# Score matmuls of two batches behind one another in the second chunk, and a new price for one batch's block, in a gated linear attention with a mixture of experts

## Chip, cores and metric

One NeuronCore of a Trainium2 chip. The metric is the time of one execution on the device in microseconds; the profile's span is some 1.7 us shorter. Verdicts use fast runs only.

## The reference

```python
# attention: B=4, H=8, S=768, D=48
f = 1 / (1 + exp(-f_logit))
for t in range(S):
    state = f[:, :, t, :, None] * state + einsum('bhd,bhe->bhde', k[:, :, t], v[:, :, t])
    y[:, :, t] = einsum('bhd,bhde->bhe', q[:, :, t], state)
# experts: x = y as (3072, 384), E=4, F=1024
p = domain_probs / (domain_probs.sum(-1, keepdims=True) + 1e-09)
out = sum(p[:, e:e+1] * (relu(x @ w1[e]) @ w2[e]) for e in range(E))
```

## The kernel before

The sequence is cut into six chunks of 128 steps. In each, the attention of four batches feeds the expert layers of the chunk. Before the program is built, a list scheduler in the kernel places every operation, with a priority and a price in microseconds, on an engine, and so fixes each engine's order.

```python
class Plan:
    ...
    def run(self):
        # the operation with the best priority that is ready and whose buffers are free goes next
        ...
rooms = {"ps_m": 4, "ps_t": 4, ...}      # PSUM banks: experts, attention

def product(c, b, j, eng): ...   # L276: gated q (j=0) or k (j=1), VectorE or GpSimd

def pe_at(c, b):                 # scores of one batch: 8 matmuls, L300
    QK = tl("QK", c, b)
    for i in range(NP):
        for r in range(2):
            rows = slice(r * P2, r * P2 + D)      # 48 rows from partition 0 or 64
            nc.tensor.matmul(out=tl("A", c, b, r)[:, i, :], lhsT=QK[rows, 1, i, :], rhs=QK[rows, 0, i, :],
                             start=True, stop=True)

def ev_at(c, b, r): ...          # VectorE masks one bank of scores, L304
def pe_y(c, b): ...              # output from scores and state, L311 and L315
def probs(c): ...                # VectorE normalises the expert weights pn, L241 to L244
def mm_h(...): ...               # first expert layer, L344; relu L350 (VectorE), L352 (ScalarE)
def mm_o(...): ...               # second expert layer, L356; ev_o leaves PSUM, scaled by pn: L363, L365, L367
    ...
        pairs = [[b] for b in range(B)] if c < 2 else [[b, b + 1] for b in range(0, B, 2)]
        for bs in pairs:
            at = P.add(f"at {c}.{bs[-1]}", {"PE": 0.4 if len(bs) == 1 else 0.66},
                       lambda e, bs=bs: [pe_at(c, b) for b in bs], slot(bs[-1], 7),
                       deps=[ET[b] for b in bs], takes=[("ps_t", "A", c, b, r) for b in bs for r in range(2)], lag=0.2,
                       frees=[("QK", c, b) for b in bs])
    ...
    done = P.run()
    for o in done:
        o.emit(o.engine)
```

## Time and profile before

| | before |
|---|---|
| time, median of 3 runs | 303.41 us (302.98 to 304.57) |
| span of the profiled run | 302.5 us |
| TensorE busy, granted clock | 97%, full |
| VectorE, ScalarE, GpSimd busy | 45%, 57%, 32% |

TensorE sets the end, so the time changes only where its stream gets shorter or waits. A group in the timeline reads: start, length, engine, line, operation, out<-in, form, count, and in brackets the idle time ahead and what ended it. Matmul ends are modelled and overlap the next start, so what a group costs is read from the start of the next one.

### The profile page before, as it was taken

The page shows a single profiled execution, that of the slowest core. Times are in us where ns is not written, and L with a number is a line of the kernel's source. Part 1 is how long each engine was busy: PE and PEld are TensorE (multiplying, and loading weights), DVE is VectorE, ACT ScalarE, POOL GpSimd, SP SyncE. Part 2 cuts the span into 40 slices and gives each one's busy share as a digit, 9 for nine tenths or more (in the row PEclk, how much of TensorE's full clock was granted, in tenths as well). Part 3 has the DMA queues.
Part 4 walks back from the last instruction along what each step waited for, and adds up shares of the span by engine and source line. Part 5 has one row for each costly group of instructions (what it writes and reads, how often), then busy time and mean ns, then how long its engine had stood idle before and what let it go on. Part 6 is the DMA issues. An engine that isn't in the chain of part 4 may idle for free.

```text
span 302.5 us, 5544 instructions
## 1 busy us (share of the span) xinstructions
PE 294.6 (97%) x2141; PEld 170.9 (56%) x2141; DVE 136.8 (45%) x269; ACT 172.1 (57%) x299; POOL 95.7 (32%) x157
## 2 busy tenths in 40 slices
PE   7898999999999999999999999999999999999995
PEld 5664555566775566556555555555556555555553
DVE  6693002789753574526364426364315253201223
ACT  5766664857776464677455575435566444475440
POOL 4584300407666047332434252622342100000000
PEclk9999999999999999999999999999999999999999
DMA  8999999963995559967799978200422201100003
GB/s 159 206 175 207 208 207 196 218 100 61 216 217 113 113 110 186 179 137 152 141 175 160 220 167 154 50 15 13 115 62 52 48 13 32 66 21 2 0 0 106
DMA packets 137355, 36.10 MB, mean 119 GB/s; under 512 B 128496, under 2 KB 135792, under 8 KB 137328
## 3 DMA queue, kind: packets, MB, share of 16 engines
q1 hardware_dynamic: 131568, 29.45, 49.8%
q0 software_dynamic: 5760, 6.29, 12.5%
q8 instruction: 17, 0.28, 0.4%
q14 instruction: 10, 0.08, 0.1%
HBM read 31.51 MB, written 4.72 MB: 120 GB/s over the span
## 4 chain that ended last, share of the span: by engine, by line
PE 90%; DMA 4%; DVE 3%; POOL 1%; ACT 1%; issue 1%; DVEq 0%; ACTq 0%; POOLq 0%
PE ps_m L356 40%; PE ps_m L344 40%; DMA w_sb<-in_moe_w_dram 3%; PE ps_t L300 2%; PE ps_t L255 1%; PE ps_t L315 1%; PE ps_t L321 1%; PE ps_t L311 1%; POOL qk L276 1%; DMA f<-in_f_logit_dram 1%; DVE qk L276 1%; PE ps_m L569 1%; PE ps_t L285 1%; DVE AT L304 0%; POOL Sf L335 0%
## 5 line engine op out<-in xcount | busy, mean ns | idle before, releaser
L344 PE MATMUL ps_m<-xT,w_sb 128*128 128x512 bf16 (+1 forms) x624 | 153.1, 363 | 1.3 <-DMA w_sb<-in_moe_w_dram 0.9
L356 PE MATMUL ps_m<-w_sb,h 128*128 128x384 bf16 x776 | 153.2, 324 | 0.0
L352 ACT ACTIVATE h<-ps_m 128x512 bf16<-128x512 f32 (+1 forms) x169 | 97.3, 577 | 98.0 <-PE ps_m L344 93.8
L356 PEld LDWEIGHTS <-h 128*128 128x128 bf16 x776 | 73.5, 98 | 58.6
L363 DVE SCALAR_TENSOR_TENSOR o<-ps_m,pn,o 128x384 f32<-128x384 f32 (+1 forms) x73 | 44.6, 611 | 107.2 <-PE ps_m L356 101.3
L344 PEld LDWEIGHTS <-w_sb 128*128 128x128 bf16 x624 | 59.5, 98 | 47.7 <-DMA w_sb<-in_moe_w_dram 1.1
L276 POOL TENSOR_TENSOR qk<-q,e 128x384 bf16<-128x384 f32 x18 | 21.6, 1204 | 64.3 <-ACT e L262 63.9
L350 DVE TENSOR_SCALAR h<-ps_m 128x512 bf16<-128x512 f32 (+1 forms) x39 | 21.9, 578 | 27.1 <-PE ps_m L344 24.2
L304 DVE TENSOR_TENSOR AT<-ps_t,mask 128x512 bf16<-128x512 f32 x48 | 30.2, 682 | 7.4 <-PE ps_t L300 7.4
L335 POOL TENSOR_TENSOR Sf<-Sf,egs 48x192 f32<-48x192 f32 x40 | 20.7, 517 | 39.9 <-DVE Sf L328 37.8
L276 POOL TENSOR_TENSOR qk<-k,e 128x384 bf16<-128x384 f32 x21 | 22.2, 1059 | 20.2 <-ACT e L264 12.9
L262 ACT ACTIVATE e<-ps_t 128x384 f32<-128x384 f32 x24 | 20.7, 864 | 4.8 <-PE ps_t L255 2.6
L328 DVE TENSOR_TENSOR Sf<-Sf,ps_t 48x192 f32<-48x192 f32 x40 | 14.0, 350 | 10.8 <-PE ps_t L321 10.0
L365 ACT ACTIVATE o<-ps_m,pn 128x384 f32<-128x384 f32 x20 | 11.6, 580 | 5.8 <-PE ps_m L356 4.3
L336 POOL CAST sb<-Sf 48x192 bf16<-48x192 f32 x40 | 13.6, 339 | 2.6
L569 PE MATMUL ps_m<-busy 128*128 128x256 bf16 x69 | 12.8, 333 | 1.3 <-DVE busy L140 1.3
L218 POOL CAST vb<-v 128x384 bf16<-128x384 f32 x18 | 9.7, 558 | 11.9 <-DMA v<-in_v_dram 9.7
L264 ACT ACTIVATE e<-ps_t 128x384 f32<-128x384 f32 x24 | 13.0, 541 | 0.0
L247 ACT ACTIVATE ex<-f 128x768 f32<-128x768 f32 (+1 forms) x14 | 10.5, 748 | 3.2 <-DMA f<-in_f_logit_dram 3.2
L315 PE MATMUL ps_t<-vb,AT 128*128 128x48 bf16 x192 | 11.4, 184 | 0.7 <-DVE vb L218 0.7
L315 PEld LDWEIGHTS <-AT 128*128 128x128 bf16 x192 | 9.8, 97 | 2.5 <-issue 0.9
L251 ACT ACTIVATE gp<-ex 128x768 bf16<-128x768 f32 (+1 forms) x14 | 10.5, 751 | 0.4
(50 smaller groups left out, 141.7 us busy)
## 6 DMA issues: line engine op xcount, KB each, us to landing
w_sb<-in_moe_w_dram POOLq DMA_DIRECT2D x8, 768.0 KB, 19.2
out_dram<-o SPq DMA_DIRECT2D x23, 192.0 KB, 2.1
f<-in_f_logit_dram SPq DMA_DIRECT2D x10, 384.0 KB, 4.2
k<-in_k_dram SPq DMA_DIRECT2D x10, 384.0 KB, 5.3
q<-in_q_dram SPq DMA_DIRECT2D x10, 384.0 KB, 5.3
v<-in_v_dram SPq DMA_DIRECT2D x10, 384.0 KB, 5.5
f<-in_f_logit_dram SPq DMA_DIRECT2D x4, 192.0 KB, 3.8
k<-in_k_dram SPq DMA_DIRECT2D x4, 192.0 KB, 4.0
```

Of the source, the lines that this page charges most:

```text
L262: nc.scalar.activation(out=e[:, 0].rearrange("t (d h) -> t h d", d=D), in_=cs[:, 0:HD].rearrange("t (i r d) -> t r i d", r=2, d=D), func=A ...
L276: engines[eng].tensor_tensor(out=tl("qk", c, b)[:, j, :, 0:D].rearrange("t (i r) d -> t i r d", r=2), in0=tl("qk"[j], c, b // 2)[:, hh(b), ...
L304: nc.vector.tensor_tensor(out=tl("AT", c, b)[:, r].rearrange("s i t -> s (i t)"), in0=tl("A", c, b, r).rearrange("s i t -> s (i t)"), in1= ...
L315: nc.tensor.matmul(out=y[:, h * D:(h + 1) * D], lhsT=AT[:, r, i, :], rhs=vb[:, h, :], start=(c == 0), stop=True, skip_group_check=True)
L328: nc.vector.tensor_tensor(out=Sf[rows, b], in0=Sf[rows, b], in1=KV[rows, :, r, :], op=ALU.add)
L335: nc.gpsimd.tensor_tensor(out=Sf[rows, b], in0=Sf[rows, b], in1=eg, op=ALU.mult)
L344: nc.tensor.matmul(out=tl("hp", c, e, fc, n0)[:, n0:n1], lhsT=w1_sb[:, e, kk, fc * 128:(fc + 1) * 128], rhs=tl("xT", c)[:, kk, n0:n1], sta ...
L350: nc.vector.tensor_relu(out=dst, in_=src)
L352: nc.scalar.activation(out=dst, in_=src, func=AF.Relu)
L356: nc.tensor.matmul(out=tl("op", c, e, nt, part)[:, cols], lhsT=tl("h", c, e)[:, fc, nt * T:(nt + 1) * T], rhs=w2_sb[:, e, fc, cols], start ...
L363: nc.vector.scalar_tensor_tensor(out=o, in0=op, scalar=pe, in1=o, op0=ALU.mult, op1=ALU.add)
L569: nc.tensor.matmul(out=spare[:, 0:256], lhsT=busy[:, 0:128], rhs=busy, start=True, stop=True)
```

## The change

It is to give the second chunk what the third to sixth already have: the scores of two batches in one block, so that TensorE changes to the 48-row mode and back twice less. A single block's price is corrected besides.

```diff
-        pairs = [[b] for b in range(B)] if c < 2 else [[b, b + 1] for b in range(0, B, 2)]
+        pairs = [[b] for b in range(B)] if c < 1 else [[b, b + 1] for b in range(0, B, 2)]
...
-            at = P.add(f"at {c}.{bs[-1]}", {"PE": 0.4 if len(bs) == 1 else 0.66}, ...
+            at = P.add(f"at {c}.{bs[-1]}", {"PE": 0.43 if len(bs) == 1 else 0.66}, ...
```

More of the change, by code (lines that the diff above doesn't have):

```diff
@@ L438, in attention @@
             ET[b], VB[b] = et, vb
-        pairs = [[b] for b in range(B)] if c < 2 else [[b, b + 1] for b in range(0, B, 2)]
+        pairs = [[b] for b in range(B)] if c < 1 else [[b, b + 1] for b in range(0, B, 2)]
         AT_ = {}
         for bs in pairs:
-            at = P.add(f"at {c}.{bs[-1]}", {"PE": 0.4 if len(bs) == 1 else 0.66}, lambda e, bs=bs: [pe_at(c, b) for b in bs], slot(bs[-1], 7),
+            at = P.add(f"at {c}.{bs[-1]}", {"PE": 0.43 if len(bs) == 1 else 0.66}, lambda e, bs=bs: [pe_at(c, b) for b in bs], slot(bs[-1], 7),
                        deps=[ET[b] for b in bs], takes=[("ps_t", "A", c, b, r) for b in bs for r in range(2)], lag=0.2,
```

## The prediction

> **What bounds the kernel now.** I read the page's busy shares, the 40 slices, the chain that ended last and the groups of instructions first, then the timeline of the stretch in which the second chunk's scores are made, and last the same stretch by engine.
>
> ```profile
> PE 294.6 (97%) x2141; PEld 170.9 (56%) x2141; DVE 136.8 (45%) x269; ACT 172.1 (57%) x299; POOL 95.7 (32%) x157
> ...
> PEclk9999999999999999999999999999999999999999
> ...
> PE 90%; DMA 4%; DVE 3%; POOL 1%; ACT 1%; issue 1%; DVEq 0%; ACTq 0%; POOLq 0%
> PE ps_m L356 40%; PE ps_m L344 40%; DMA w_sb<-in_moe_w_dram 3%; PE ps_t L300 2%; PE ps_t L255 1%; PE ps_t L315 1%; PE ps_t L321 1%; PE ps_t L311 1%; POOL qk L276 1%; DMA f<-in_f_logit_dram 1%; DVE qk L276 1%; PE ps_m L569 1%; PE ps_t L285 1%; DVE AT L304 0%; POOL Sf L335 0%
> ```
>
> TensorE is the bound: 97% busy, 90% of the chain, full granted clock in every slice, while VectorE and ScalarE are about half busy. Of the chain 80% is the two expert layers (L344, L356); the score matmuls (L300) are 2%. The first expert matmul starts at 23.83 us, 0.85 us late behind a weight DMA, and from there TensorE runs to within 3 us of the end of the 302.5 us span. So time is won or lost only where TensorE's stream gets shorter or gets a hole after 23.8 us.
>
> How that stream is made up must be read from the starts of the matmuls, as their ends overlap. In the timeline of TensorE (start, length, line, form, count), ordinary expert groups of four 128x384 matmuls follow at 0.65 us: 4 x 384 columns at 2.4 columns per ns is 0.640 us, so almost nothing is lost. Round the score matmuls it is otherwise:
>
> ```profile
> 60.22 0.81 PE L356 MATMUL ps_m<-w_sb,h 128*128 128x384 bf16 x4
> 60.97 0.40 PE L300 MATMUL ps_t<-QK 48*128 48x128 bf16 x8
> 61.30 0.82 PE L344 MATMUL ps_m<-xT,w_sb 128*128 128x512 bf16 x3
> 62.05 0.40 PE L300 MATMUL ps_t<-QK 48*128 48x128 bf16 x8
> ...
> 101.01 0.81 PE L356 MATMUL ps_m<-w_sb,h 128*128 128x384 bf16 x4
> 101.75 0.62 PE L300 MATMUL ps_t<-QK 48*128 48x128 bf16 x16
> 102.31 0.82 PE L344 MATMUL ps_m<-xT,w_sb 128*128 128x512 bf16 x3
> ```
>
> The first four lines are the second chunk, one batch (8 matmuls) at a time; the last three are the third chunk, which already issues two batches (16) together. The group of 60.22 should hand over at 60.87 and does so at 60.97: 0.10 us lost on entering. Eight score matmuls then take 61.30 - 60.97 = 0.33 us and sixteen take 102.31 - 101.75 = 0.56 us, so eight more cost 0.23 us, and 0.10 us of each block is a fixed loss on leaving. In single starts: the last expert matmul ahead of the block occupies 258 ns where 160 ns is its stream, and the last score matmul 148 ns where 53 ns is. So 98 ns on the way in and 95 ns on the way out, at nearly every block of this kind in the trace (94 to 99 ns).
>
> **What the Trainium skill says.** "TensorEngine Tiling (Array Packing)", Key Properties: changing the tiling mode, as opposed to the tile, drains the engine. The score matmuls contract over 48 rows that start at partition 0 or 64, so they run as two row tiles; everything round them uses the whole array. The trace agrees, and gives the price, 98 + 95 ns. "TensorE: Matmul & The Clock Gate", Part 3 (The mechanism): matmuls on different row groups run concurrently, their starts some 4 ns apart. The trace agrees: starts come in pairs 3 ns apart, pairs 56 ns apart, so 8 matmuls cost 4 x 56 = 0.22 us. "PSUM — Partial Sum Buffer", The four PSUM rules: one matmul output is at most one bank of 512 fp32. A score tile (4 heads x 128 fp32) is just that, and a batch has two, so a pair fills all four of the rotating banks that the attention part has. "SBUF — State Buffer", two separate sides: VectorE and GpSimd share a port pair under an exclusive lock; I use this only in a rival below.
>
> **The change, part by part.** No instruction is added or removed: the 32 score matmuls of the second chunk stay, in two blocks of 16 where there were four of 8 (at 60.97, 62.05, 73.62 and 76.62 us). In time:
>
> Four single blocks: 4 x (0.10 + 0.33) = 1.72 us of TensorE. Two paired: 2 x (0.10 + 0.56) = 1.32 us. Gain 0.40 us, which is two changes of mode, 2 x (98 + 95) = 0.39 us. All four old blocks stand apart in the stream with other matmuls between them, so no drain was shared before. All of it lies on the path, as TensorE is the chain there. 0.40 of 303.4 us is 0.13%.
>
> The second edited number (0.40 to 0.43 us for a single block) emits nothing. It is a price in the planner that fixes each engine's order before the program is built, and is just the 0.10 + 0.33 measured above. It is left to the first chunk only, where it may shift warm-up matmuls or their number; that part ends in the 0.85 us wait for weights, which should swallow it.
>
> What moves: scores of batch 0 wait for batch 1's copies, which end at 61.43 us, so the pair takes about the place of the second block, 62 us. In the third chunk VectorE begins the first masking 0.70 us after the block's start (102.45 - 101.75), since it waits for the whole pair. Here that gives 62.7, against 61.40 before, and four maskings last 2.48 us, to 65.2 against 63.88. Batch 0's output moves by some 1 us; batch 1's, issued at 65.09 before, by 0.1 to 0.2. The expert work fed by these two batches starts at 69.42 us, while its last input copy ended at 67.82, a slack of 1.6 us. In the second half the copies of batches 2 and 3 end at 72.89 and 75.77 us, so the pair goes out at about 76.0: batch 2 is later by 2.4 us, but batch 3, which ends the half, is earlier by 0.6 on TensorE. Masking then runs 76.7 to 79.2, against 78.34 before, the last output 79.2 against 78.98, and the last input copy 81.5 against 81.29. The experts need it at about 82.3. So neither half should open a hole for want of data.
>
> **Rivals.** First, a hole made by the reshuffled order. Between 69 and 84 us TensorE already loses more than the change is worth:
>
> ```profile
> 70.39 0.49 PE L344 MATMUL ps_m<-xT,w_sb 128*128 128x256 bf16 x3
> 71.19 0.66 PE L285 MATMUL ps_t<-ident,qk 128*112 128x128 bf16 x8 [0.30 <-DVE qk L276]
> 71.68 1.47 PE L344 MATMUL ps_m<-xT,w_sb 128*128 128x256 bf16 x12
> 73.26 0.43 PE L285 MATMUL ps_t<-ident,qk 128*112 128x128 bf16 x4
> ```
>
> The transposes of batches 2 and 3 wait for VectorE's products: 0.47 us of TensorE at 70.6 and 0.27 at 72.9 (one product took 1.63 us beside one on GpSimd, where others took 0.85). At 82.2 and 83.1 another 0.51 and 0.20 go, waiting for PSUM to be emptied. That is 1.45 us which depends on which operation the planner put where; a new order can lose half of it, or add as much. For: VectorE will have two unbroken maskings of 2.5 us, and the 128x256 relus of the second half (0.38 to 0.42 us each, a new one every 0.33 us) then fall to ScalarE alone. Against: the planner knows these costs, and the third chunk has lived with such a block. Worth -0.7 to +1.0 us; the time would be 302.3 to 304.0.
>
> Second, the four banks. A pair can start only when all four are free, and it holds the last until 79 us, so transposes, outputs and state matmuls cannot slip in. If the half ends more than 0.8 us later than I worked out, TensorE stands: +0.5 to +1.5 us, 303.5 to 304.5. Against: at 61 and 76 us nothing else wants these banks, as the next chunk's first use comes at 81.37.
>
> Third, the drain is won but handed back: the wait for PSUM at 82 us is set by VectorE and ScalarE, so a TensorE that comes 0.4 us earlier waits 0.4 longer. The time would be 303.4. The third chunk onward has few holes, so what is won by 86 us is kept.
>
> **Range and chances.** 303.41 - 0.40 gives 303.0. I take off nothing more, as the reshuffle can go either way and its two sides nearly cancel. Repeats of the kernel before spread from 302.98 to 304.57, so a median of few runs is uncertain by about 0.5 us; with the reshuffle's 0.7 us this gives 302.1 to 304.2 for 8 in 10. A change of 2% is 6.1 us, four times all the holes listed; only a gross accident of the planner makes that. Faster 0.01, same 0.98, slower 0.01.
>
> **What would show it.** Right: L300 in the second chunk appears twice, x16, each taking 0.56 us with 0.10 lost ahead of it; everything after 90 us stands 0.2 to 0.6 us earlier; the busy time of other engines is unchanged; the first expert matmul stays at 23.8 us. Wrong: a wait of TensorE between 62 and 86 us longer than the 1.45 us of before, x8 blocks that stay next to each other, or a first expert matmul that moves by more than 0.2 us. The prediction fails outright if the new order carries on into the third chunk and delays its attention part, which I could not see from here.

## The result

| | before | changed |
|---|---|---|
| time, median of 6 runs | 303.55 us (302.90 to 304.57) | 303.58 us (302.81 to 303.90) |
| ratio of fast runs, 95% interval | 1 | 0.9996 (0.9973 to 1.0019) |
| span of the profiled run | 302.5 us | 301.3 us |
| first expert matmul starts | 23.83 us | 23.23 us |
| stretch | 275.34 us | 274.71 us |

A ratio is the mean time of one kernel's fast runs over that of the other's of the same rounds, so not quite the ratio of the medians. The timing resolves about 0.7 us, so it neither shows nor excludes a gain of 0.4 us. The two traces do.

First the page of the changed kernel: busy shares and the chain that ended last.

```profile
PE 292.1 (97%) x2110; PEld 170.9 (57%) x2141; DVE 134.1 (44%) x266; ACT 173.7 (58%) x302; POOL 95.9 (32%) x157
...
PE 75%; DMA 11%; SPq 4%; POOL 3%; issue 3%; DVE 1%; ACT 1%; POOLq 0%; ACTq 0%
```

The engines are as busy as before. (31 records of matmuls are missing in this trace, 2110 for 2141, which is why TensorE's busy time seems to fall; all weight loads are there.) The chain has less TensorE because up to 69 us it was traced back through other work, most of it loads of the weights and of k, not because TensorE works less. Next the timeline of TensorE in the changed kernel, the two blocks and what follows the largest wait:

```profile
61.66 0.62 PE L300 MATMUL ps_t<-QK 48*128 48x128 bf16 x16
62.22 2.12 PE L356 MATMUL ps_m<-w_sb,h 128*128 128x384 bf16 x12
...
75.23 0.62 PE L300 MATMUL ps_t<-QK 48*128 48x128 bf16 x16
75.79 0.50 PE L344 MATMUL ps_m<-xT,w_sb 128*128 128x256 bf16 x3
...
80.91 2.76 PE L356 MATMUL ps_m<-w_sb,h 128*128 128x384 bf16 x16
84.40 3.37 PE L344 MATMUL ps_m<-xT,w_sb 128*128 128x256 bf16 x27 [0.73 <-DVE o L367]
```

There are two blocks of 16, each 0.56 us from its start to the next start, as predicted. But the planner also put three groups of expert matmuls (62.22) behind the first pair where there had been one, and at 83.5 us TensorE now waits 0.89 us in one piece (the group of 80.91 ends its stream at 83.51). So two things moved, the modes and the waits. I added all losses of TensorE of more than 45 ns in the stretch, from the matmuls' starts: changes of mode fell from 2.31 to 1.94 us, other waits went from 1.65 (without one for a load at 163 us) to 1.60 us. Is the gain then the modes alone, as predicted? The experiments say no.

### The profile page after: what moved, and what is told of

It reads as the page before. It is cut to its first block, busy times and chain, and to the rows that moved or that the text cites. A ratio compares the mean times of both kernels' runs of the same rounds, so it can differ in the third digit from the quotient of the medians.

```text
span 301.3 us, 5508 instructions
## 1 busy us (share of the span) xinstructions
PE 292.1 (97%) x2110; PEld 170.9 (57%) x2141; DVE 134.1 (44%) x266; ACT 173.7 (58%) x302; POOL 95.9 (32%) x157
## 4 chain that ended last, share of the span: by engine, by line
PE 75%; DMA 11%; SPq 4%; POOL 3%; issue 3%; DVE 1%; ACT 1%; POOLq 0%; ACTq 0%
PE ps_m L356 34%; PE ps_m L344 33%; DMA w_sb<-in_moe_w_dram 8%; SPq L222 4%; DMA k<-in_k_dram 2%; POOL qk L276 2%; PE ps_t L300 2%; POOL w_sb L229 1%; PE ps_t L315 1%; PE ps_t L255 1%; PE ps_t L311 1%; DMA f<-in_f_logit_dram 1%; PE ps_m L569 1%; PE ps_t L321 1%; PE ps_t L285 0%
## 5 line engine op out<-in xcount | busy, mean ns | idle before, releaser
L352 ACT ACTIVATE h<-ps_m 128x512 bf16<-128x512 f32 (+1 forms) x172 | 99.7, 580 | 97.3 <-PE ps_m L344 91.1
L344 PE MATMUL ps_m<-xT,w_sb 128*128 128x512 bf16 (+1 forms) x593 | 150.2, 362 | 2.4 <-DVE o L367 0.7
L350 DVE TENSOR_SCALAR h<-ps_m 128x512 bf16<-128x512 f32 (+1 forms) x36 | 19.1, 555 | 19.6 <-PE ps_m L344 19.2
L315 PE MATMUL ps_t<-vb,AT 128*128 128x48 bf16 x192 | 11.4, 184 | 0.7 <-DVE vb L218 0.7
L315 PEld LDWEIGHTS <-AT 128*128 128x128 bf16 x192 | 9.8, 97 | 2.3 <-issue 0.9
```

The source lines that it names most:

```text
L315: nc.tensor.matmul(out=y[:, h * D:(h + 1) * D], lhsT=AT[:, r, i, :], rhs=vb[:, h, :], start=(c == 0), stop=True, skip_group_check=True)
L344: nc.tensor.matmul(out=tl("hp", c, e, fc, n0)[:, n0:n1], lhsT=w1_sb[:, e, kk, fc * 128:(fc + 1) * 128], rhs=tl("xT", c)[:, kk, n0:n1], sta ...
L350: nc.vector.tensor_relu(out=dst, in_=src)
L352: nc.scalar.activation(out=dst, in_=src, func=AF.Relu)
```

## The experiments

**How the stretches compare.** Three things unrelated to an edit enter a stretch, and each is visible in its trace. If the first expert matmuls come late, the clock can still be halved for some of them: 128x512 matmuls start 427 ns apart, not 216. The second chunk's prefix sums (L255, near 54 us) can wait for a load of the gate. And near 163 us the fourth chunk's first expert matmul sometimes waits; which load is behind that I did not find. The last column takes these three out. Four kernels ran once only and have no ratio, so the stretch is all there is of them: the two with a pair joined by hand, pairing without the price, and price without the pairing.

| kernel | stretch, us | halved clock | loads | left |
|---|---|---|---|---|
| before, two traces | 275.34, 275.13 | 0 | 0.19, 0 | 275.15, 275.13 |
| changed, two traces | 274.71, 274.69 | 0 | 0 | 274.71, 274.69 |
| changed, whole-array matmul inside pairs | 277.13 | 0 | 0 | 277.13 |
| changed, 48-row matmul inside pairs | 275.18 | 0 | 0.14 | 275.04 |
| before, first pair joined | 275.87 | 0.43 | 0 | 275.44 |
| the same, filled | 275.81 | 0 | 0.85 | 274.96 |
| pairing without the price | 276.47 | 1.08 | 0 | 275.39 |
| price without the pairing | 274.83 | 0 | 0.42 | 274.41 |
| nothing paired | 277.45 | 1.24 | 0 | 276.21 |
| changed, normalised early, two traces | 273.56, 273.56 | 0 | 0 | 273.56, 273.56 |
| before, normalised early | 275.36 | 0 | 0.20 | 275.15 |

### Noise: both kernels again

No edit.

> The kernel before, unchanged, for the noise. I measure the stretch from the start of the first expert matmul to the start of the last matmul on TensorE: 275.34 us in the first trace of this kernel. If that stretch is fixed by the order of the program, it repeats within 0.1 us, while the start of the first expert matmul (23.83 us, behind a weight DMA) moves by some 0.5 us from run to run and makes the spread of the total. If TensorE's stream itself varies, the stretch moves by 0.5 us or more. Ratio to itself 1.000 within 0.002.

> The changed kernel, unchanged. Its stretch was 274.71 us, 0.63 us shorter than before, and its first expert matmul started 0.60 us earlier. Theory: the 0.63 repeats (within 0.1), since it is 0.4 of mode changes and 0.2 of smaller waits, and the 0.60 does not, since no instruction of TensorE ahead of the first 415 weight loads and matmuls differs. The ratio should then be 0.998, between 0.996 and 1.000. Rival: both came from the weight DMA's luck and the ratio is 1.000.

Ratios 0.9998 (0.9970 to 1.0025) and 0.9990 (0.9965 to 1.0016). The stretches repeat within 0.02 us once the wait at 163 us is set aside, so the order of the program fixes them: 275.13 against 274.69, 0.44 us. The 0.63 of the first pair of traces held 0.19 of that chance wait. The start of the first expert matmul went from 23.83 to 22.42 us in the kernel before, so it is chance; up to the second chunk TensorE's orders in both kernels are the same. The theory holds on the repeat and on the start; that the 0.63 would repeat was wrong.

The profile of the changed kernel fell into a slow run: its first expert matmul came at 32.70 us, with a stretch of 274.69 all the same. That is 9.47 us later than in its fast trace, and the run took 9.45 us longer (312.45 against 303.00). What was slow shows in the waits. ScalarE's timeline around the last cast of v, first in the slow trace of the changed kernel, then in the fast repeat of before:

```profile
28.45 0.51 ACT L216 CAST vb<-v 128x384 bf16<-128x384 f32 x1 [9.64 <-DMA v<-in_v_dram]
```

```profile
18.74 0.51 ACT L216 CAST vb<-v 128x384 bf16<-128x384 f32 x1 [0.48 <-DMA v<-in_v_dram]
```

The last load of v landed 9.7 us later. In each of the three late traces (this one, pairing alone, and the first of the early normalisation) that cast waited 8.0 to 10.0 us. The lower mean clock of these runs (0.984 to 0.988) follows from TensorE's idle time: "TensorE: Matmul & The Clock Gate", Part 1, says that an idle window halves the clock, and in the slow trace above the granted clock was 0.50 from 24 to 28 us, when TensorE did nothing.

### The price of a change of mode

```diff
-  lambda e, bs=bs: [pe_at(c, b) for b in bs]
+  lambda e, bs=bs: [(b != bs[0] and nc.tensor.matmul(out=tl("A", c, b, 0)[:, 0, 0:64],
+      lhsT=busy[ROWS, 0:128], rhs=busy[ROWS, 0:64], start=True, stop=True), pe_at(c, b)) for b in bs]
   # ROWS = : (whole array) or 0:48 (the mode of the scores)
```

> The order of the changed kernel, but between the two batches of each of the 10 pairs one dummy matmul of 64 columns over the whole array, into a score tile that is overwritten at once. Theory (the price is the change of mode): each adds 98 + 95 ns and 27 ns of stream, 2.2 us in the stretch, to 276.9 us, and 0.7% in time. Rival (pairing gains only through the new order): each adds its 27 ns, 0.3 us in all.

> As the run before it, but the dummy matmul uses 48 rows, so that TensorE stays in the mode of the score matmuls. Theory: 10 x 27 ns to 10 x 55 ns, 0.3 to 0.55 us in the stretch, to 275.0 to 275.3 us. Rival (any foreign matmul between the batches costs the 0.19 us, whatever its mode): 2.2 us, as with the whole array.

Against the stretch of the changed kernel, 274.70 us, the whole-array matmul added 2.43 us, 0.24 for each pair; the time over that of the kernel before was 1.0061 (1.0031 to 1.0091). The 48-row matmul added 0.34 us, 0.03 each, at 1.0000 of the kernel before (0.9971 to 1.0029). The timelines of TensorE at the first pair, whole array first:

```profile
61.85 0.40 PE L300 MATMUL ps_t<-QK 48*128 48x128 bf16 x8
62.18 0.20 PE L443 MATMUL ps_t<-busy 128*128 128x64 bf16 x1
62.31 0.40 PE L300 MATMUL ps_t<-QK 48*128 48x128 bf16 x8
```

```profile
61.21 0.40 PE L300 MATMUL ps_t<-QK 48*128 48x128 bf16 x8
61.45 0.19 PE L443 MATMUL ps_t<-busy 48*128 48x64 bf16 x1
61.45 0.41 PE L300 MATMUL ps_t<-QK 48*128 48x128 bf16 x8
```

Eight score matmuls take 0.33 us ahead of the whole-array matmul and 0.24 ahead of the other; the former then takes 0.13 us where its stream is 0.027. So it is the change of mode that costs, about 0.2 us there and back, and not any foreign matmul. That step of the prediction is shown with the order held fixed.

### One pair joined by hand

In the kernel before, in its own order:

```diff
     done = P.run()
+    # the expert group between "at 1.0" and "at 1.1" goes ahead of both; the first masking goes behind both
+    done[i:j + 1] = between + [at_1_0, at_1_1] + [ev_at0_1_0]
```

> The order that the planner made for the kernel before, kept, except that the one group of expert matmuls which stood between the score blocks of batches 0 and 1 of the second chunk goes ahead of both, so that these two are one block. Nothing else moves. Theory: the stretch from the first expert matmul to the last matmul shrinks by one change of mode, 0.19 us, from 275.13 (the repeat of before) to 274.94, with the waits at 69 to 85 us unchanged. Rival (pairing delays batch 0 by 1 us and TensorE waits for it later): no gain, 275.1 or more, and a new wait of TensorE after 63 us.

```diff
+    done.insert(y, done.pop(k))    # besides: the next expert group k ahead of the output y of batch 0
```

> The kernel before with the first pair joined, as in the run that lost 0.50 us to a wait inside batch 0's output, and one more edit of the order: the next group of expert matmuls (0.65 us) goes between the pair and that output. Theory: the wait was there because joined scores are masked later while the output kept its place; with 0.65 us of work ahead of it the wait closes, the 0.19 us of the mode change is kept, and the stretch is 274.94 us (to 275.05; plus 0.2 us for each full group of matmuls under the low clock at the start, if the weights come late). Rival (the late masking delays the following steps anyway): the wait comes back further on and the stretch is 275.2 or more.

Joined only, the stretch grew by 0.31 us, against the theory. The timeline of TensorE shows the wait that the rival named:

```profile
66.35 0.21 PE L311 MATMUL ps_t<-sb,QK 112*128 112x96 bf16 x1
66.40 0.19 PE L315 MATMUL ps_t<-vb,AT 128*128 128x48 bf16 x1
66.92 0.20 PE L315 MATMUL ps_t<-vb,AT 128*128 128x48 bf16 x1 [0.33 <-DVE AT L304]
```

The second of two L315 starts 0.52 us after the first instead of 0.03: batch 0's second masking is not done, since masking begins only behind the whole pair. Filled with one expert group the wait is gone:

```profile
62.00 0.62 PE L300 MATMUL ps_t<-QK 48*128 48x128 bf16 x16
62.55 1.47 PE L356 MATMUL ps_m<-w_sb,h 128*128 128x384 bf16 x8
63.86 0.21 PE L311 MATMUL ps_t<-sb,QK 112*128 112x96 bf16 x1
63.91 0.21 PE L315 MATMUL ps_t<-vb,AT 128*128 128x48 bf16 x2
```

The raw stretch, 275.81 us, is beyond what either theory expected, because two waits of 0.43 and 0.42 us for loads fell into it, outside the edited part. Measured across that part alone, from the second block of transposes (L285) to the next prefix sums (L255): before (repeat) 58.37 to 66.38, 8.01 us; joined 63.30 to 71.60, 8.30; filled 60.16 to 67.99, 7.83. So joining a pair gains the 0.18 us of the mode and loses 0.5 us to later masking unless other work is put between; in the changed kernel the planner did that with three groups.

### Pairing and price apart

```diff
 # pairing only                                  # price only
-  ... if c < 2 else ...                         -  {"PE": 0.4 if len(bs) == 1 else 0.66}
+  ... if c < 1 else ...                         +  {"PE": (0.43 if c < 1 else 0.4) if len(bs) == 1 else 0.66}
```

> The pairing alone, with the single block of the first chunk still priced at 0.40 us. Theory: the second edited number only reshuffles; stretch 274.7 plus or minus 0.3 us, with 10 blocks of scores after the first chunk and 1.94 us of mode changes. If the price were what makes the new order good, the stretch is 275.0 or more.

> The price alone, 0.43 us in the first chunk and 0.40 in the second, no pairing. Theory: 12 blocks and 2.32 us of mode changes as before, stretch 275.13 plus or minus 0.2 us. If the price had a part in the gain, 274.9 or less.

Both went against the theory. Of the table's last column:

| stretch left, us | price 0.40 | price 0.43 in the first chunk |
|---|---|---|
| not paired | 275.13 | 274.41 |
| paired | 275.39 | 274.70 |

**Pairing costs 0.26 and 0.29 us; the price gains 0.72 and 0.69 us.** The two add up to the 0.43 us that the whole change gains. With the price alone, the traces show a single difference of order in the whole kernel: in the second half of the second chunk VectorE and GpSimd swap the two products of one batch. In all else VectorE's 269 and GpSimd's 157 instructions, ScalarE's 299 and TensorE's 2141 weight loads follow in the same order as in the repeat of before (by line, name and form; the traces leave batch numbers out, so that like operations of two batches, or the transposes of q and k, cannot be told apart). GpSimd's and VectorE's timelines, before and then with the price alone:

```profile
69.42 1.00 POOL L276 TENSOR_TENSOR qk<-k,e 128x384 bf16<-128x384 f32 x1 [9.19 <-ACT e L264]
69.50 1.63 DVE L276 TENSOR_TENSOR qk<-q,e 128x384 bf16<-128x384 f32 x1
```

```profile
69.01 1.19 POOL L276 TENSOR_TENSOR qk<-q,e 128x384 bf16<-128x384 f32 x1 [8.90 <-ACT e L262]
69.41 1.20 DVE L276 TENSOR_TENSOR qk<-k,e 128x384 bf16<-128x384 f32 x1
```

VectorE's product ends last both times, 0.71 us behind GpSimd's before (71.13 against 70.42) and 0.41 with the swap (70.61 against 70.20). The shortest products on VectorE in the trace of before took 0.85 us for q and 0.55 for k. Next the transposes that need it, on TensorE; those of before are in the prediction (71.19, with the wait ahead):

```profile
70.30 0.49 PE L344 MATMUL ps_m<-xT,w_sb 128*128 128x256 bf16 x3
70.67 0.65 PE L285 MATMUL ps_t<-ident,qk 128*112 128x128 bf16 x8
```

The three expert matmuls now take 0.37 us to the next start where they took 0.80 (70.39 to 71.19). The wait of 0.47 us, and the one of 0.26 that followed, are gone: from the prefix sums to the next score block it took 5.81 us before (66.38 to 72.19, repeat) and 5.08 with the price, 0.73 less. In the kernel with both edits these waits fell to 0.34 us.

Pairing alone brings its 0.39 us less of modes, and larger waits near 93 us. TensorE, then VectorE, in the trace of pairing alone (which is 10 us late from its slow start):

```profile
93.70 0.49 PE L344 MATMUL ps_m<-xT,w_sb 128*128 128x256 bf16 x3 [0.75 <-ACT h L352]
94.03 0.81 PE L356 MATMUL ps_m<-w_sb,h 128*128 128x384 bf16 x4
95.90 1.36 PE L344 MATMUL ps_m<-xT,w_sb 128*128 128x256 bf16 x11 [1.05 <-DVE o L367]
```

```profile
93.42 0.81 DVE L242 TENSOR_SCALAR psm<-psm 128x4 f32<-128x4 f32 x1
94.27 0.18 DVE L243 RECIPROCAL psm<-psm 128x4 f32<-128x4 f32 x1
94.48 0.71 DVE L244 TENSOR_TENSOR pn<-pt,psm 128x16 f32<-128x16 f32 x1
95.22 0.62 DVE L367 TENSOR_SCALAR o<-ps_m,pn 128x384 f32<-128x384 f32 x1
```

The first of these waits was ended by a relu of ScalarE, the second by an output that came behind the normalisation. By their starts they are 0.91 and 1.22 us, 2.13 together; at the same place the kernel before lost 0.77 us, the price alone 0.78, both edits 1.16. This trace is a single one, with 1.08 us taken off for the halved clock, so of its size I am sure to perhaps 0.1 us.

That the price gains about the same in both rows of the table is chance, as it acts in different places. Not paired, it ends the waits for products, 0.73 us. Paired, those waits are there with the price (0.34 us) and not without it, and what falls are the waits near 83 us (93 in the late trace), from 2.13 to 1.16 us.

### The wait at 83 us

The four operations that normalise the expert weights have 4 or 16 elements per partition and took 0.17 to 0.20 us each before, on VectorE:

```profile
81.53 0.17 DVE L242 TENSOR_SCALAR psm<-psm 128x4 f32<-128x4 f32 x1
81.95 0.20 DVE L244 TENSOR_TENSOR pn<-pt,psm 128x16 f32<-128x16 f32 x1
```

In the changed kernel these two took 0.46 and 0.71 us. VectorE and GpSimd in its trace:

```profile
82.28 0.46 DVE L242 TENSOR_SCALAR psm<-psm 128x4 f32<-128x4 f32 x1
82.78 0.18 DVE L243 RECIPROCAL psm<-psm 128x4 f32<-128x4 f32 x1
82.99 0.71 DVE L244 TENSOR_TENSOR pn<-pt,psm 128x16 f32<-128x16 f32 x1
83.73 0.62 DVE L367 TENSOR_SCALAR o<-ps_m,pn 128x384 f32<-128x384 f32 x1
```

```profile
81.53 1.18 POOL L276 TENSOR_TENSOR qk<-q,e 128x384 bf16<-128x384 f32 x1
82.68 0.99 POOL L276 TENSOR_TENSOR qk<-k,e 128x384 bf16<-128x384 f32 x1
```

The two slow ones end at 82.74 and 83.70 us, each 0.03 us after a product of the next chunk on GpSimd (82.71 and 83.67). "SBUF — State Buffer", SBUF: two separate sides, says that a VectorE operation that needs the port pair shared with GpSimd and an operation of GpSimd exclude each other, and the later one blocks for a whole instruction. The trace agrees by these end times; the other two operations (0.17 and 0.18 us, beside the same products) were not held. In the kernel before the same operations fell beside short ones of GpSimd. Only after 83.70 can an output leave PSUM and give TensorE its bank. To test this I moved the four operations in the fixed order:

```diff
     done = P.run()
+    early = next(o for o in done if o.name == "probs 1")
+    done.remove(early)
+    done.insert([o.name for o in done].index(X), early)    # X: "ev_at0 1.2" (changed), "ev_at0 1.3" (before)
```

> The changed kernel's order, kept, but the four small VectorE operations that normalise the expert weights of the second chunk go ahead of the maskings of batches 2 and 3, where VectorE stood idle for 1.5 us. Theory: the largest wait of TensorE that is left (0.88 us, near 83 us) is for these: no first output of the chunk can leave PSUM until they are done, at 83.70 us. It closes, and the stretch goes from 274.70 to between 273.7 and 274.0. Rival (VectorE and ScalarE cannot empty PSUM any faster there): 0.5 us or more of it stays, 274.3 to 274.7. In time the gain is 0.2 to 0.3%, so near the noise.

> The changed kernel with the early normalisation once more, on another day's chip state, as its first timing fell among many slow runs. Its stretch was 273.56 us, 1.58 us below before, which is 0.52% of the time. If that is all that it does, the stretch repeats within 0.1 us and the ratio is 0.995, between 0.992 and 0.998; if the 0.992 of the first time was real, it lies below 0.993 again.

> The same move in the order of the kernel before (ahead of the maskings of batch 3, where VectorE was idle for 1.3 us). Theory: its waits of 0.52 and 0.20 us near 81 us have the same cause and close in part: stretch from 275.13 to between 274.4 and 274.7. The changed kernel with the same move should be shorter by 0.4 us of mode changes and the rest of its own wait. Rival: 275.0 or more.

In the changed kernel the stretch fell by 1.15 us, to 273.56 in both traces, more than expected, as the smaller waits that followed closed too. The fast second trace, on TensorE:

```profile
81.64 2.76 PE L356 MATMUL ps_m<-w_sb,h 128*128 128x384 bf16 x16
84.24 2.02 PE L344 MATMUL ps_m<-xT,w_sb 128*128 128x256 bf16 x17
```

The 16 matmuls need 2.56 us of stream and take 2.60. The ratios to the kernel before are 0.9921 (0.9880 to 0.9962) and 0.9958 (0.9873 to 1.0043), both wide because many runs of those rounds were slow; the stretch says 1.57 us, 0.5%. It has the shortest stretch of all versions here; the price alone with the same move, which starts from a shorter stretch (274.41 us), was not run.

In the kernel before the move gained nothing (275.15). VectorE was done earlier there, but the two waits of 0.51 and 0.20 us became one of 0.78 us, released by a relu of ScalarE, which stood behind four exponentials:

```profile
84.30 1.80 PE L344 MATMUL ps_m<-xT,w_sb 128*128 128x256 bf16 x15 [0.62 <-ACT h L352]
```

So in this kernel the normalisation alone does not set the wait, and my expectation was wrong.

### Nothing paired

```diff
-        pairs = [[b] for b in range(B)] if c < 2 else [[b, b + 1] for b in range(0, B, 2)]
+        pairs = [[b] for b in range(B)]          # single block at 0.43
```

> No chunk pairs its batches: planned anew with a single block priced at 0.43 us throughout, 20 blocks after the first chunk where the kernel before had 12 and the changed kernel has 10. Theory: 8 more changes of mode there and back than before, 8 x 0.193 = 1.5 us, so a stretch of 276.7 us, plus or minus 0.7 for the waits of a new order; time ratio to before 1.005. Rival (the planner fills what the modes cost, or the new order decides): the stretch is within 0.5 us of 275.1 or beyond 277.5.

The stretch left is 276.21, 1.08 us over before, inside what the theory gave. Changes of mode went from 2.32 to 3.85 us, by 1.52 for 8 blocks more; other waits fell by 0.6 us from 1.63. The ratio, 1.0008 (0.9962 to 1.0054), does not resolve it. Here too the modes cost what they should and the new order moved the rest.

## Why the prediction was right, and where it was not

- **Total.** Predicted 303.0 us in 302.1 to 304.2 and "same" with 0.98; measured 303.58 and "same". The timing cannot tell 0.13% from nothing.
- **Modes.** "Gain 0.40 us, which is two changes of mode": right. The loss at score blocks fell by 0.39 us, and the whole-array matmul put it back at 0.24 us each.
- **The second number.** "The second edited number (0.40 to 0.43 us for a single block) emits nothing ... that part ends in the 0.85 us wait for weights, which should swallow it": wrong. It emits nothing, and TensorE's order up to the second chunk is unchanged, but later the planner's order differs, and that is worth 0.7 us, more than the modes: without the pairing, all of it, as far as the traces tell the orders apart, by one swap of two products between VectorE and GpSimd. I looked for its effect only where the priced operation stands.
- **The reshuffle.** "The reshuffle can go either way and its two sides nearly cancel": they did cancel, to 0.05 us in the sum of waits, but between two effects of 0.6 to 0.7 us that I had not separated: new waits from pairing and lost waits from the price. In the repeats of both kernels the modes fell from 2.32 to 1.93 us, the waits for products from 0.72 to 0.34, and the waits near 83 us rose from 0.77 to 1.15. That the net gain of 0.43 us is close to my 0.40 is therefore partly luck. Without the price the same pairing would have lost 0.26 us.
- **Delays.** "Neither half should open a hole for want of data": it held in the changed kernel, but only because the planner moved other work behind the pair; with the order kept a wait of 0.50 us opened. The first rival, named for VectorE's two maskings, was right in kind; its cause near 83 us was the normalisation beside GpSimd's products. The third rival, that the wait for PSUM there hands the gain back, came true in size (0.38 us more) but not in cause. Of the second, the four banks, the changed kernel's trace shows nothing: between 62 and 86 us no loss of more than 45 ns stands at the scores, outputs or state matmuls, except for the modes.
- **The start.** "The first expert matmul stays at 23.8 us": the program's does, the run's does not; it went from 22.4 to 33.7 us in the traces, by when loads land.

Open: how 0.03 us of price in the first chunk leads the planner to that swap, and which differences of order make the price gain with the pairing, where many differ. It is one greedy schedule against another; nothing here says that the truer price is better elsewhere.

## What to carry to other kernels

Where a kernel orders itself by prices, a change of grouping or price is a change of the whole order behind it: count what the edit saves, then list the waits of the bound engine before and after, and test the edit once with the order frozen. For effects under the noise, compare a stretch of the trace that starts after the loads, and set aside the waits that differ between two traces of one kernel. Small operations that gate the emptying of PSUM are worth moving to where their engine is idle, as a test: here the move gained 1.15 us in one order and nothing in the other.

## What the Trainium skill lacked or had wrong

- "TensorEngine Tiling (Array Packing)", Key Properties, says that a change of mode drains the engine, without a price: here 98 ns on entering and 95 ns on leaving for blocks of 128-column matmuls, 108 ns on entering behind a single 64-column one; 0.24 us for an excursion of one 64-column matmul.
- "SBUF — State Buffer", on the shared port pair, is right and was borne out to the end time: a VectorE operation of 4 elements per partition took 0.46 or 0.81 us instead of 0.17 beside a GpSimd product. What the page I used does not bring out is that such small operations can hold up TensorE, here for 0.89 us.
- No page that I used has the late start seen here: the last load of v ahead of the first weight loads landed 12.1 to 15.1 us after its issue in the three late traces and 4.0 to 8.6 us in the eleven others. It was issued 0.3 to 0.7 us ahead of the first weight load in the late ones and 0.5 to 1.1 in the others, so nearness does not explain it; the cause is open. In the two traces of slow runs this, and not a slower clock throughout, made the time.
